# Strided and local attention with a gated feed-forward layer on one core: early loads held back to 1.1 MB under way, and fewer filler products

## The chip, the cores and the metric

The kernel runs on one core of one Trainium2 chip. Its engines are TensorE (PE; its weight loads are shown as PEld), VectorE (DVE), ScalarE (ACT), GpSimd (POOL) and SyncE (SP), which here issues all transfers between HBM and the core's memory. The metric is the device time of one execution in microseconds (us).

## The reference

For 8 batches and 8 heads of 576 positions by 64, the reference computes softmax attention under a mask, four heads with a local band of 32 positions, four with a stride of 32; the heads' outputs, put side by side as x (576 x 512 for each batch), go through a gated layer:

```python
scores = np.where(masks, (q @ k.T) / 8, -1e9)
attn = softmax(scores)                       # per head
x = concat_heads(attn @ v)                   # 576 x 512 per batch
h = np.maximum(x @ w_in, 0.0)                # 512 x 1024
u, v = h[..., :512], h[..., 512:]
v_n = (v - mean(v)) / np.sqrt(var(v) + 1e-6)
v_s = einsum("ts,bsd->btd", w_spatial, v_n) + b_spatial[None, :, None]
out = (u * v_s) @ w_out                      # 512 x 512
```

w_in and w_out arrive as 64-bit floats, the rest as 32-bit.

## The kernel before

All large products are made of two-part operands: each number is split into a rounded part and a rest, and three products of the parts stand for one. So each weight and each activation passes through a short preparation before PE can use it. A weight of 64 bits is loaded as raw words, and the helper `words` (from line 773) turns them into 32-bit numbers in three steps: ACT scales the upper words (L789), POOL or DVE takes three bits of the lower ones (L798), DVE joins them (L806). Then `rnd` writes the rounded part (L412 on ACT, L414 on POOL) and `rest` the remainder (L422). The spatial weights wsp and wtail need only the last two.

A batch has four attention tiles of two heads each. For each tile PE makes scores (L507 for local heads, L650 for strided ones), DVE and ACT the softmax (L527 to L588, L675 to L704), the turned probabilities are copied to ptl or pts, PE multiplies them with v (L617, L720), and ACT and DVE write the result x in two parts (L434, L422). Per batch PE then makes the v half (L957) and the u half (L999) of the first layer, the spatial product (L1079, with its tail in L1091 and L1092) and the last product (L1168).

The order of all this is not written by hand. Each step is entered into a list with a key and a cost, `Program.order` (line 190) plays the list through with costs and latencies, and gives each engine's order and a planned time in ns for each step. The first eight attention tiles and all weights are entered first, so that the loads of the first 50 to 70 us are q, k, v, w_in, w_spatial and w_out mixed. Below, transfers are numbered by their place in SP's order, from 1; the first 53 are issued within the first 66 us of the profile.

Each engine works through its instructions in order and waits at each for the semaphores that it names. A transfer adds to one of eight semaphores, DMAHW0 to DMAHW7, taken in turn: transfer n uses number (n − 1) mod 8. Before a semaphore is taken again, SP waits for the landing of the transfer that had it last, the eighth before; so at most eight are under way.

`Program.fillers` (line 318) looks in the planned first 110 us for places at which PE would stand idle for over 0.7 us ahead of certain steps. There `emit` puts products of a 32x256 tile of zeros (L1349) ahead of the step, into the tile that the step will overwrite: a share, WARM_SHARE, of the idle time divided by 427 ns, rounded down.

```python
if gap > WARM_GAP:
    found[n] = int(WARM_SHARE * gap / WARM_COST)
```

Of the kernel before, what the change touches and what calls it, by code (L numbers as in the profile page):

```python
# [56 lines left out]
    "p": (2.79, 10.51, 0.21,),  # L57
    "b": (25.62, -1.03, 29.44, -12.2, 10.78, 11.69, 33.63, 25.64, -64.18, 15.47, 14.89,),
}
WARM_END, WARM_GAP, WARM_COST, WARM_COLS, WARM_SHARE = 110000.0, 700.0, 427.0, 256, 0.8  # L60
PE_MASKED, APART = (0, 1, 2, 3), (0, 1)
OTHER_BANK = (1, 2, 3)
FETCHED, FETCH_COST = 100.0, 32.0
SLOWED = ((0.3, 0.15), (0.45, 0.6), (0.9, 0.8))
DMA_RATE, DMA_ISSUE, DMA_LAG, DMA_TAIL, TABLE_LOAD = 370.0, 470.0, 1500.0, 500.0, 1280.0
PROD = ((0, 0), (0, 1), (1, 0))
BLOCKS = ("a11", "a12", "a22", "s1", "s2", "s3", "s4")
# [4 lines left out]
PE, ACT, DVE, POOL, DMA = "tensor", "scalar", "vector", "gpsimd", "sync"  # L72
# [77 lines left out]
class Program:  # L150
# [39 lines left out]
    def order(self):  # L190
# [17 lines left out]
        def shared(n, e, at, cost):  # L208

            if e in self.port.get(n, ()):  # L210
                since, until, share, _ = held_by[peer[e]]
                if since <= at < until:
                    both = min(until - at, cost)
                    slow = SLOWED[max(share, self.share[n])]
                    return (slow[0] * both, slow[1] * both) if e == DVE else (slow[1] * both, slow[0] * both)
# [115 lines left out]
                free = at + cost  # L331
        return found

    def emit(self, nc, warm):
        issued = self.order()
        fillers = self.fillers(issued)
        for _, n, e in issued:
            if e == PE and fillers.get(n):
                warm(self.spare[n][1], fillers[n])
            self.ops[n][2](getattr(nc, e))  # L340


def pe_cost(m, n):
# [4 lines left out]
def attention_moe(ctx, tc, qT, kT, ks, vl, vs, cst, eye, w_in, w_out, wsp, wtail, out):  # L348
    nc = tc.nc
# [4 lines left out]
    prog = Program()  # L354
# [898 lines left out]
    starts, knots, at = [], [(0.0, NHP)], 0.0  # L1253
# [98 lines left out]
                start=True, stop=True,  # L1352
            )

    prog.emit(nc, warm)


def _layout(q, k, v, w_in, w_spatial, b_spatial, w_out):
# [75 lines left out]
```

## Time and profile before

| | |
|---|---|
| time, median of 3 runs (lowest, highest) | 520.41 us (519.15, 520.59) |
| the profiled execution: time | 519.78 us |
| the profiled execution: span, first to last instruction | 517.7 us |
| PE busy | 499.6 us, 97% of the span |
| DVE busy | 363.0 us, 70% |
| ACT busy | 267.4 us, 52% |
| POOL busy | 129.0 us, 25% |
| bytes moved | 52.65 MB, 102 GB/s on average |
| mean granted PE clock | 0.98 |

Busy times come from one profiled execution. A timeline row has the start in us, the duration, the engine, the line, the operation, output<-inputs by the program's names without buffer numbers, the shapes and a count; in brackets stands how long the engine was idle before it, and what ended that. A row of SPq is the issue of a transfer. In the view of one tile, the row "DMA to landing" gives the time from issue to landing. L12 is line 12 of the kernel file. The changed file is longer: its lines are ten further down from `emit` on, so that L442, L789 and L1079 are L452, L799 and L1089 there.

### The profile page before, as it was taken

What the parts mean: (1) busy time and instruction counts of PE and PEld (TensorE: products, weight loads), DVE (VectorE), ACT (ScalarE), POOL (GpSimd) and SP (SyncE); (2) the same over time, 40 slices, a digit from 0 to 9 for tenths busy, and PEclk for the clock granted to TensorE, in tenths of its full rate; (3) what the DMA queues carried; (4) which work ended last, traced back from release to release, by engine and by line L of the source; (5) the groups of instructions that cost most, each with busy time, mean ns of one, the idle gap of its engine ahead of it and who ended that gap; (6) DMA issues with size and microseconds to landing.
All of it is one profiled execution on the core that took longest, in us unless ns stands there. A gap on an engine that the chain in (4) does not pass through costs nothing.

```text
span 517.7 us, 14663 instructions
## 1 busy us (share of the span) xinstructions
PE 499.6 (97%) x5884; PEld 459.3 (89%) x5884; DVE 363.0 (70%) x1093; ACT 267.4 (52%) x825; POOL 129.0 (25%) x245
## 2 busy tenths in 40 slices
PE   6779889999999999999999999999999999999997
PEld 3558779979999899998999899998999889998997
DVE  2899989969479747896369764897457861676156
ACT  5786765568554476456336276366446252233222
POOL 3355864043212121312102111233102120102000
PEclk9689979999999999999999999999999999999999
DMA  8897323454024322262023422063011300020002
GB/s 274 307 343 268 125 83 90 149 164 151 2 79 151 118 79 81 85 180 84 11 69 121 148 80 80 1 209 113 1 56 53 123 1 1 1 80 13 1 1 91
DMA packets 26243, 52.65 MB, mean 102 GB/s; under 512 B 3136, under 2 KB 11584, under 8 KB 26176
## 3 DMA queue, kind: packets, MB, share of 16 engines
q1 hardware_dynamic: 26176, 51.72, 30.3%
q8 instruction: 46, 0.75, 0.6%
q14 instruction: 21, 0.17, 0.1%
HBM read 42.27 MB, written 9.44 MB: 100 GB/s over the span
## 4 chain that ended last, share of the span: by engine, by line
PE 89%; DVE 4%; DMA 2%; ACT 2%; SPq 1%; POOL 1%; issue 1%; POOLq 0%
PE m L1079 20%; PE m L957 18%; PE m L1168 18%; PE m L999 18%; PE po L720 4%; PE po L617 3%; PE s L507 3%; PE s L650 2%; PE m L1091 2%; PE m L1092 2%; DMA k<-kT 1%; SPq L442 1%; DMA x<-wsp 1%; PE po L1349 1%; DVE w_in_sb L422 0%
## 5 line engine op out<-in xcount | busy, mean ns | idle before, releaser
L1079 PE MATMUL m<-wsp_sb,vn 128*128 128x288 f32 x768 | 113.3, 300 | 4.3 <-DVE wsp_sb L422 4.3
L1079 PEld LDWEIGHTS m<-wsp_sb,vn 128*128 128x128 f32 x768 | 107.3, 192 | 5.4 <-DVE wsp_sb L422 4.6
L999 PE MATMUL m<-x,w_in_sb 128*128 128x288 f32 x768 | 105.3, 297 | 0.0
L999 PEld LDWEIGHTS m<-x,w_in_sb 128*128 128x128 f32 x768 | 103.4, 188 | 1.2
L957 PE MATMUL m<-w_in_sb,x 128*128 128x512 f32 (+1 forms) x408 | 99.5, 399 | 0.0
L957 PEld LDWEIGHTS m<-w_in_sb,x 128*128 128x128 f32 (+1 forms) x408 | 74.5, 186 | 19.0 <-DVE x L422 0.2
L1168 PE MATMUL m<-g,w_out_sb 128*128 128x288 f32 x384 | 56.9, 298 | 0.0
L414 POOL TENSOR_SCALAR ptl<-pc 32x64 f32<-32x64 f32 (+3 forms) x89 | 37.9, 426 | 64.7 <-DVE pc L588 24.2
L1168 PEld LDWEIGHTS m<-g,w_out_sb 128*128 128x128 f32 x384 | 52.3, 188 | 1.0 <-ACT vv L434 0.3
L422 DVE TENSOR_TENSOR x<-po,x 128x288 fp32r<-128x288 f32 x64 | 27.6, 447 | 36.3 <-ACT x L434 35.6
L1101 DVE TENSOR_TENSOR u<-m,u 128x288 f32<-128x288 f32 x64 | 28.1, 453 | 30.9 <-PE m L1092 30.7
L564 ACT ACTIVATE pl<-pl,ml 128x64 f32<-128x64 f32 (+1 forms) x140 | 47.0, 339 | 4.7 <-DVE ml L544 4.3
L915 ACT ACTIVATE vv<-m 128x512 f32<-128x512 f32 (+1 forms) x37 | 22.0, 596 | 45.7 <-PE m L957 39.6
L412 ACT CAST g<-u 128x288 fp32r<-128x288 f32 x46 | 19.2, 434 | 50.2 <-DVE u L1101 49.0
L933 POOL TENSOR_TENSOR bn<-bn,sel 128x1 f32<-128x1 f32 (+1 forms) x37 | 21.1, 575 | 95.0 <-DVE bn L928 77.0
L1013 ACT ACTIVATE u<-m 128x288 f32<-128x288 f32 x64 | 25.7, 408 | 35.0 <-PE m L999 34.6
L1168 PE MATMUL m<-vn,w_out_sb 128*128 128x288 f32 x288 | 42.6, 297 | 0.0
L920 DVE BATCH_NORM_STATS2 bn<-vv 128x6 f32<-128x512 f32 (+1 forms) x37 | 25.3, 683 | 21.0 <-ACT vv L915 20.5
L1168 PEld LDWEIGHTS m<-vn,w_out_sb 128*128 128x128 f32 x288 | 39.5, 188 | 0.4
L434 ACT CAST x<-po 128x288 fp32r<-128x288 f32 x64 | 24.7, 397 | 26.2 <-PE po L617 14.4
L412 ACT COPY ptl<-pc 32x64 f32<-32x64 f32 (+3 forms) x103 | 35.7, 346 | 4.7 <-DVE pc L588 2.6
L422 DVE TENSOR_TENSOR g<-u,g 128x288 fp32r<-128x288 f32 x64 | 27.0, 449 | 7.9 <-ACT g L412 6.2
(131 smaller groups left out, 726.6 us busy)
## 6 DMA issues: line engine op xcount, KB each, us to landing
q<-qT SPq DMA_DIRECT2D x30, 295.0 KB, 4.2
outT<-o SPq DMA_DIRECT2D x48, 144.0 KB, 2.7
v_raw<-vs SPq DMA_DIRECT2D x13, 512.0 KB, 4.2
v_raw<-vl SPq DMA_DIRECT2D x16, 384.0 KB, 3.7
k<-kT SPq DMA_DIRECT2D x16, 304.0 KB, 4.5
kbd<-ks SPq DMA_DIRECT2D x32, 144.0 KB, 4.6
outT<-vv SPq DMA_DIRECT2D x16, 144.0 KB, 3.7
vn<-w_in SPq DMA_DIRECT2D x4, 512.0 KB, 4.5
```

The lines of the kernel that those rows point to most:

```text
L412: eng.copy(dst(), src())
L414: eng.tensor_scalar(dst(), src(), 1.0, 0.0, op0=ALU.mult, op1=ALU.add)
L422: eng.tensor_tensor(dst(), src(), f32(hi()), op=ALU.subtract)
L434: eng.copy(dst(), src())
L564: eng.activation(p_sb()[:m, u, :], src, AF.Exp, bias=st()[:m, u : u + 1], scale=SCALE if masked else -1.0, **total,)
L920: lambda eng: eng.bn_stats(bn()[:m, 0:6], v()[:m]), [(v,)], [(bn,)],
L957: eng.matmul(v_ps()[:m, :], x_at(kt)[:, a, :], w_in_sb[:, w, kt, HF:], start=(n == 0 and i == 0), stop=(n == NT - 1 and i == 2),)
L999: eng.matmul(u_ps()[:, :HS], w_in_sb[:, w, kt, f * P : (f + 1) * P], xs[NHP * b + kt]()[:, a, r], start=(n == 0 and i == 0), stop=(n == NT ...
L1013: lambda eng, u=u, f=f, u_ps=u_ps: eng.activation(u()[:, f * HS : (f + 1) * HS], u_ps()[:, :HS], AF.Relu),
L1079: eng.matmul(s_ps()[:, :HS], vn()[:, a, kt, fs], wsp_sb[:, w, kt, r], start=(kt == 0 and i == 0), stop=False,)
L1101: lambda eng, ug=ug, s_ps=s_ps: eng.tensor_tensor(ug(), s_ps()[:, :HS], ug(), op=ALU.mult),
L1168: eng.matmul(o_ps()[:, :HS], w_out_sb()[:, b_at, w, kk, a * P : (a + 1) * P], at(j, kk), start=first and kk == 0 and i == 0, stop=kk == 1 ...
```

## The change

Two things are changed. First, WARM_SHARE goes from 0.8 to 0.4. Second, `emit` keeps a list of the transfers sent so far. For each transfer that the plan puts into the first 70 us it goes backwards through the list, the transfer itself included, as long as the sizes come to at most GATE, 1.1 million bytes. The transfer before those it makes a dependency: the new transfer is issued only when that one has landed. No step changes its engine or its place.

```diff
-WARM_END, WARM_GAP, WARM_COST, WARM_COLS, WARM_SHARE = 110000.0, 700.0, 427.0, 256, 0.8
+WARM_END, WARM_GAP, WARM_COST, WARM_COLS, WARM_SHARE = 110000.0, 700.0, 427.0, 256, 0.4
...
+GATE, GATE_END = 1.1e6, 70000.0
...
-    def emit(self, nc, warm):
+    def emit(self, nc, warm, wait):
         issued = self.order()
         fillers = self.fillers(issued)
-        for _, n, e in issued:
+        sent = []
+        for at, n, e in issued:
             if e == PE and fillers.get(n):
                 warm(self.spare[n][1], fillers[n])
-            self.ops[n][2](getattr(nc, e))
+            made = self.ops[n][2](getattr(nc, e))
+            if e == DMA and at < GATE_END:
+                sent.append((made, self.bytes[n]))
+                under_way, k = 0, len(sent)
+                while k and under_way + sent[k - 1][1] <= GATE:
+                    k -= 1
+                    under_way += sent[k][1]
+                if 0 < k < len(sent):
+                    wait(made, sent[k - 1][0])
...
-    prog.emit(nc, warm)
+    def wait(later, earlier):
+        tc.add_manual_dep(
+            later.ins if hasattr(later, "ins") else later, (earlier.ins if hasattr(earlier, "ins") else earlier).name,
+            mybir.DependencyInfo(mybir.DependencyClass.Sync, mybir.DependencyReason.DATA),
+            reason="transfers under way",
+        )
+
+    prog.emit(nc, warm, wait)
```

SP's order at the start, transfers 5 to 14, before. Names are the buffers that are filled (vn and u hold raw words of w_in here, w_out_sb holds an early q) and the inputs; 128x1024 are four-byte words, so w_in's and vs's transfers have 512 KB, vl's 384, kT's 304, qT's 295, wsp's and wtail's 288, ks's 144:

```order
L442 DMA vn_101<-w_in 128x1024
L442 DMA kbd<-ks 64x576 [waits Pool_49]
L442 DMA kbd<-ks 64x576
L442 DMA q_123<-qT 128x590
L442 DMA k_134<-kT 128x608 [waits DMAHW0_49]
L442 DMA v_raw_140<-vl 128x768 [waits DMAHW1_49]
L442 DMA q_176<-qT 128x590 [waits DMAHW2_49]
L442 DMA k_181<-kT 128x608 [waits DMAHW3_49]
L442 DMA v_raw_220<-vl 128x768 [waits DMAHW4_49]
L442 DMA u_225<-w_in 128x1024 [waits DMAHW5_49]
```

The same ten transfers in the changed kernel:

```order
L452 DMA vn_101<-w_in 128x1024 [waits DMAHW1_49]
L452 DMA kbd<-ks 64x576 [waits Pool_49]
L452 DMA kbd<-ks 64x576
L452 DMA q_119<-qT 128x590 [waits DMAHW4_49]
L452 DMA k_130<-kT 128x608 [waits DMAHW0_49]
L452 DMA v_raw_136<-vl 128x768 [waits DMAHW6_49]
L452 DMA q_172<-qT 128x590 [waits DMAHW7_49,DMAHW2_49]
L452 DMA k_177<-kT 128x608 [waits DMAHW3_49,DMAHW0_49]
L452 DMA v_raw_216<-vl 128x768 [waits DMAHW1_49]
L452 DMA u_221<-w_in 128x1024 [waits DMAHW5_49,DMAHW3_49]
```

Nothing has changed its place. Transfer 5 now waits for transfer 2 (DMAHW1), 8 for 5 (DMAHW4), 10 for 7, 11 for 8, 12 for 9 (DMAHW0), 13 for 10 and 14 for 12 (DMAHW3); where two are named, the other is the eighth before, as it was.

SP's order further on, transfers 37 to 44, before (g holds raw words of w_out, xt and v_raw the values v, x raw spatial weights):

```order
L442 DMA g_649<-w_out 128x1024 [waits DMAHW4_49,DVE_49,Pool_49]
L442 DMA k_657<-kT 128x608 [waits DMAHW6_49,DMAHW5_49,PE_49]
L442 DMA q_673<-qT 128x590
L442 DMA kbd<-ks 64x576 [waits DMAHW7_49]
L442 DMA kbd<-ks 64x576 [waits DMAHW0_49]
L442 DMA xt_696<-vs 128x1024 [waits DMAHW1_49]
L442 DMA x_328<-wsp 128x576 [waits DMAHW2_49]
L442 DMA g_736<-w_out 128x1024 [waits DMAHW3_49,DVE_49,Pool_49]
```

And in the changed kernel (the two kbd rows print as one):

```order
L452 DMA g_643<-w_out 128x1024 [waits DMAHW2_49,DVE_49,Pool_49]
L452 DMA k_651<-kT 128x608 [waits DMAHW5_49,DMAHW3_49,PE_49]
L452 DMA q_667<-qT 128x590 [waits DMAHW4_49]
L452 DMA kbd<-ks 64x576 x2
L452 DMA xt_690<-vs 128x1024 [waits DMAHW6_49,DMAHW1_49]
L452 DMA x_322<-wsp 128x576 [waits DMAHW7_49]
L452 DMA g_730<-w_out 128x1024 [waits DMAHW1_49,DVE_49,Pool_49]
```

Transfer 37 now waits for 35 (DMAHW2), 39 for 37 (DMAHW4), 42 for 39 (DMAHW6) and 44 for 42 (DMAHW1).

PE's order ahead of the first value product of a strided tile (s are scores, po the product's tile, pts the turned probabilities), before:

```order
L507 MATMUL s_128<-k_181,q_176 32x64
L507 MATMUL s_131<-k_181,q_176 32x64
L1349 MATMUL po_292<-zeros 32x256 x3
L720 MATMUL po_292<-pts,xt_87 64x4x18 [waits DMAHW1_49,Activation_49,Pool_49]
L720 MATMUL po_292<-pts,xt_87 64x4x18 x7
```

And in the changed kernel:

```order
L517 MATMUL s_124<-k_177,q_172 32x64
L517 MATMUL s_127<-k_177,q_172 32x64
L1359 MATMUL po_288<-zeros 32x256
L730 MATMUL po_288<-pts,xt_87 64x4x18 [waits DMAHW1_49,Activation_49,Pool_49]
L730 MATMUL po_288<-pts,xt_87 64x4x18 x7
```

Here three products on zeros become one. At the start of the program eight become four; there are no others.

## The prediction

> **What bounds the kernel now.** I read the page first, then the busy times by stage, then PE's timeline around the seam between the stages, then ACT's, POOL's and DVE's timelines for the instructions that consume what was loaded, and last single transfers from issue to landing. The page gives the span, and the rate of the transfers in 40 slices of 12.9 us each:
>
> ```profile
> span 517.7 us, 14663 instructions
> ...
> GB/s 274 307 343 268 125 83 90 149 164 151 2 79 151 118 79 81 85 180 84 11 69 121 148 80 80 1 209 113 1 56 53 123 1 1 1 80 13 1 1 91
> ```
>
> The first four slices move about 300 GB/s, all later ones at most 209. The change touches the stage in which memory is asked for most. The profiled execution took 519.78 us for this span, so 2.1 us lie around it; the median of the three runs shown is 520.41, 0.6 above. My sum is made against 519.78.
>
> The stages, from the table of busy times (stretch and its length, then each engine's busy time with its count, granted clock, share of the DMA engines, GB/s):
>
> ```profile
> 0.00:17.00 17.00, 10.35 (x235) 6.47 (x236) 5.09 (x16) 9.83 (x23) 5.20 (x15) 0.81 0.88 306
> 17.00:53.40 36.40, 32.77 (x518) 25.99 (x517) 34.87 (x86) 27.90 (x78) 20.16 (x33) 0.90 0.83 292
> 53.40:67.20 13.80, 9.54 (x63) 8.15 (x61) 13.80 (x43) 10.62 (x34) 11.95 (x15) 0.93 0.36 127
> 67.20:517.70 450.50, 446.94 (x5071) 418.66 (x5071) 309.21 (x952) 219.09 (x692) 91.71 (x184) 0.99 0.24 78
> ```
>
> After 67.2 us PE is busy for 446.9 of 450.5 us: whatever delays the start of that stage delays the end, and there is no idle time in which to win it back. Before it, DVE is the full engine: 34.9 of 36.4 us, then 13.8 of 13.8. The seam itself, in PE's timeline:
>
> ```profile
> 62.64 0.29 PE L1079 MATMUL m<-wsp_sb,vn 128*128 128x288 f32 x1
> 67.21 3.01 PE L1079 MATMUL m<-wsp_sb,vn 128*128 128x288 f32 x11 [4.28 <-DVE wsp_sb L422]
> ```
>
> PE stands idle for 4.28 us until DVE has made wsp_sb. So the question is by how much the change moves DVE's work before 67.2 us, and that work starts from loaded data. These instructions consume loads first (start, duration, engine, line):
>
> ```profile
> 26.36 0.67 ACT L789 ACTIVATE g<-g 128x512 f32<-128x512 f32 x1
> 34.22 0.68 ACT L789 ACTIVATE u<-u 128x512 f32<-128x512 f32 x1
> 38.41 0.67 ACT L789 ACTIVATE vn<-vn 128x512 f32<-128x512 f32 x1
> 43.91 0.67 ACT L789 ACTIVATE g<-g 128x512 f32<-128x512 f32 x1
> 51.88 0.70 ACT L789 ACTIVATE g<-g 128x512 f32<-128x512 f32 x1
> 57.21 0.66 ACT L412 CAST wt_b<-x 128x576 fp32r<-128x576 f32 x1
> 52.48 0.67 POOL L798 TENSOR_SCALAR g<-g 128x512 int32<-128x512 uint8 x1
> 53.36 1.17 DVE L806 SCALAR_TENSOR_TENSOR g<-g 128x512 int32<-128x512 int32 x1
> ```
>
> They are the users of transfers 21, 29, 33, 37, 44 and 49 (numbered as SP issues them); POOL's and DVE's rows are the next steps on transfer 44.
>
> **The change, part by part.** *The wait.* A transfer may now be issued only when it and those still unlanded come to at most 1.1 MB, 1,074 KB of 1,024 bytes. So what counts is how long a transfer takes from issue to landing with little ahead of it. Single transfers that were issued into an idle queue, or nearly so:
>
> ```profile
> L442 SPq DMA_DIRECT2D w_out_sb<-qT x1: 387/387/387, 0.7 to 0.7; - x1
> DMA to landing us min/median/max: 3.0/3.0/3.0
> ...
> L442 SPq DMA_DIRECT2D g<-w_out x1: 327/327/327, 64.1 to 64.1; - x1
> DMA to landing us min/median/max: 3.5/3.5/3.5
> ...
> L442 SPq DMA_DIRECT2D kbd<-ks x1: 477/477/477, 22.1 to 22.1; - x1
> DMA to landing us min/median/max: 2.4/2.4/2.4
> ...
> L442 SPq DMA_DIRECT2D q<-qT x1: 328/328/328, 89.0 to 89.0; - x1
> DMA to landing us min/median/max: 3.4/3.4/3.4
> ...
> L442 SPq DMA_DIRECT2D v_raw<-vs x1: 328/328/328, 215.4 to 215.4; - x1
> DMA to landing us min/median/max: 4.6/4.6/4.6
> ...
> L442 SPq DMA_DIRECT2D xt<-vs x1: 416/416/416, 1.2 to 1.2; - x1
> DMA to landing us min/median/max: 3.8/3.8/3.8
> ```
>
> So 295 KB take 3.0 us (3.4 at worst), 512 KB 3.5 (4.6 at worst), 144 KB 2.4. While the queue was full it moved this much:
>
> ```profile
> 12.00:20.00 8.00, 5.28 (x122) 2.86 (x110) 5.88 (x17) 4.72 (x19) 2.15 (x4) 0.50 1.03 405
> ```
>
> At 405 GB/s, 405 thousand bytes per us, 512 KB need 1.3 us and 295 KB 0.75: about 2.2 us of every lone landing is not movement. With up to eight transfers under way, as before, those 2.2 us are hidden behind other transfers. With 1,074 KB they are mostly not, since the sizes fit badly: 512+304+295 is 1,111, and 512+512+144 is 1,168.
>
> The new waits can be followed by hand. I go through the order of issue, adding sizes backwards until they pass 1,074 KB, and keep only the transfers that wait for one another in a row. Transfer 2 (512 KB) lands at 1.2 + 3.8 = 5.0 us. Transfer 5 (512 KB) waits for it: 8.5. Transfer 8 (295) waits for 5: 11.5; 9 (304), issued right behind it, lands 0.8 later: 12.3. Transfer 12 (304) waits for 9: 15.3; 14 (512) for 12: 18.8; 16 (295) for 14: 21.8; 19 (512) for 16: 25.3; 21 (512) for 19: 28.8. Then 24, 26 and 29 (512 each): 32.3, 35.8, 39.3; 31 (304): 42.3; 33 (512): 45.8; 35 (304): 48.8; 37 (512): 52.3; 39 (295): 55.3; 42 and 44 (512 each): 58.8 and 62.3. From transfer 5 on that is eleven links of 3.5 us, six of 3.0 and the 0.8, 57.3 us on top of 5.0. Between the landings of 12 and 44 lie 11.3 MB, so the rate falls to 11.3 MB / 47 us = 240 GB/s, where the table has 292.
>
> Set against the users: transfer 21 comes at 28.8 for an ACT instruction that now starts at 26.4 (2.4 late), 29 at 39.3 for 34.2 (5.1 late), 33 at 45.8 for 38.4 (7.4), 37 at 52.3 for 43.9 (8.4), 44 at 62.3 for 51.9 (10.4). The lateness grows at each, so none is a consequence of the one before: the transfers set the pace, and ACT, POOL and DVE, which take their instructions in order, stand still behind each. Behind ACT's waiting instruction stand the evacuations of x and the copies of ptl and pts, for which PE waits; behind SP's waiting issue stand the later loads alone, since the stores of results come after the gated stretch.
>
> At transfer 44 the path leaves the queue. POOL starts on it 62.3 − 52.5 = 9.8 us later, and DVE's L806 with it. From there DVE has 13.8 us of work in 13.8 us, so PE's restart at 67.2 moves by the same 9.8. Transfer 49 (waits for 46, which waits for 44) comes still a little later for wt_b, but ACT has 10.6 busy of 13.8 us there and makes it up. PE's work ahead of the seam moves too and ends 4.28 us before it, which covers a PE that runs some of it at a lower clock.
>
> The rows of a lone landing scatter upwards only. If about one in five of the eleven large links takes 4.6 instead of 3.5, that adds 11/5 × 1.1 = 2.4. I take 9.8 + 2.4 = 12.2 us. Bounds: the 144 KB row has 2.4 − 0.36 of movement, 2.0 instead of 2.2 us; with that all 17 links come 0.17 shorter, 2.9 in all, and the delay is 6.9. With half of the links at their longest (5.5 × 1.1 + 3 × 0.4 = 7.3) it is 17.1.
>
> The Trainium skill (DMA: Bandwidth & Descriptors, section "Anatomy of one DMA — SWDGE (gpsimd) path") fits a DMA as 2.0 us plus its bytes at 436 GB/s, for another issuing path than SP's. By that a 512 KB link would be an estimated 3.2 us and a 295 KB link 2.7, 17 × 0.3 = 5.1 us less, and the time would be about 524.5 without the one-in-five; the trace's own rows, 3.5 and 3.0, are higher and I go by them.
>
> *The products on zeros.* Eleven become five: eight to four at the start, three to one ahead of the first value products (the counts are rounded down). PE's row of the second group, what follows it, and the makers of pts:
>
> ```profile
> 16.78 2.77 PE L1349 MATMUL po<-zeros 128*32 128x256 f32 x6
> 19.48 1.88 PE L720 MATMUL po<-pts,xt 128*64 128x72 f32 x32
> ...
> 15.62 0.92 POOL L414 TENSOR_SCALAR pts<-pc 32x288 f32<-32x288 f32 x2 [7.84 <-DVE pc L704]
> ...
> 16.04 0.86 ACT L412 COPY pts<-pc 32x288 f32<-32x288 f32 x2
> ...
> 20.75 0.40 ACT L434 CAST x<-po 128x288 fp32r<-128x288 f32 x1 [0.64 <-PE po L720]
> 21.41 0.40 ACT L434 CAST x<-po 128x288 fp32r<-128x288 f32 x1 [0.25 <-PE po L720]
> ```
>
> pts is complete at 16.9, so the three products (2.77 us, two rows each) hold L720 back by about 2.5 us; with one, 1.8 us of that go. I cost the gain at nothing, because ACT, which evacuates L720's result, then waits for transfer 21 until 28.8 in any case. Without that cover it would be worth the 0.64 + 0.25 = 0.9 us that ACT idles there. The four products dropped at the start lie in a wait for loads. That PE's clock may be lower for longer, bounded by the 0.50 of the row 12 to 20, also falls into waits.
>
> Sum: 519.78 + 12.2 − 0 = 532.0 us.
>
> **The rivals.** *Faster: landings come sooner because less is under way.* Transfer 16 needed three times as long as a lone one of its size, behind up to seven others, and PE waited for a k:
>
> ```profile
> L442 SPq DMA_DIRECT2D w_out_sb<-qT x1: 706/706/706, 10.0 to 10.0; - x1
> DMA to landing us min/median/max: 9.4/9.4/9.4
> ...
> PE s L507 <- DMA k<-kT: 1.3, 1, 1.3
> ```
>
> If the time that is not movement is itself made by the crowd, a queue with 1.1 MB lands each as soon as its bytes are moved, PE's early loads come earlier, and L720 too. It decides if a 512 KB link costs less than 2.9 us: the 9.8 us spread over 17 links are 0.58 each. Then the waits are free, the products give 0.9 and PE's wait for k at most 1.3: 519.78 − 2.2 = 517.6 us. Against it: the lone rows above have no crowd and none is under 3.5. The Trainium skill says something of this kind (same page, section "Latency and other measured facts"): HBM access takes 0.2 us on average and 2 at high load, so that a lighter load means a smaller fixed cost. The lone rows do not bear that out.
>
> *No change: the slack takes it.* Not every load is used as it lands; ACT rounds one of the last gated ones, transfer 51, only here:
>
> ```profile
> 65.58 0.67 ACT L412 CAST wsp_sb<-x 128x576 fp32r<-128x576 f32 x1
> ```
>
> If the links come out near 2.9 us, the users above get their data about when they get it now, and the seam holds: 519.8 ± 1. Against it: five users in a row are late by growing amounts, and the lone rows lie above 2.9.
>
> *Slower still: every link at its long end.* 11 × 1.1 + 6 × 0.4 = 14.6 on top of 9.8: 544 us. For it: in the gated stretch one or two other transfers are always being issued and moved; against it: half of the lone rows sit at the short end.
>
> That the wait is not in the program is no rival, since SP's listing has it.
>
> **How the numbers follow.** A measurement of this kernel can tell about 0.3% (1.6 us) from no change. My forecast, 532.0, gets 0.85; the longer tail 0.08; no change 0.03; the faster rival 0.04. The range runs from the short links (519.78 + 6.9 = 526.7, rounded down to 526) to half of them long (519.78 + 17.1 = 536.9, rounded up to 538). Slower by over 0.3%: 0.85 + 0.08 = 0.93.
>
> **What would show it.** In the changed kernel's profile the first five slices should stand near 240 GB/s and the sixth should still be full; transfer 44 should land near 62 to 65 us; ACT should wait for a DMA ahead of each L789 (L799 there); PE's stage of the spatial products should start near 79 instead of 67.2 and last 450 us as before. I am wrong if 512 KB land in under 3 us there, if ACT's waits on loads do not grow from one to the next, or if PE starts that stage before 70.

## The result, and the profile after

| kernel | median | lowest and highest of 6 runs | profiled run | its span |
|---|---|---|---|---|
| before | 519.14 us | 517.61 to 520.59 | 519.78 us | 517.7 us |
| changed | 535.04 us | 533.55 to 535.77 | 535.77 us | 533.9 us |

The ratio is 1.0302, with a 95% interval of 1.0277 to 1.0326: the change makes the kernel 15.9 us slower. The forecast was 532.0 us, in a range of 526 to 538.

The changed kernel's page, its span and its rate of transfers in 40 slices of 13.3 us:

```profile
span 533.9 us, 14639 instructions
...
GB/s 223 212 231 216 199 195 114 79 153 154 116 2 99 168 108 85 32 116 221 1 77 3 257 41 50 66 109 205 0 55 0 169 2 1 1 56 34 1 1 88
```

The first four slices stood near 300 GB/s before and stand near 220 now, and the stretch of heavy loading reaches to the sixth slice, some 80 us, where it was four slices. The stages; the first two are cut at the same times as before, the last at 82.40 us, 0.7 us ahead of the seam (length, busy time of PE, weight loads, DVE, ACT and POOL with counts, granted clock, DMA share, GB/s):

```profile
0.00:17.00 17.00, 8.70 (x154) 5.65 (x155) 5.01 (x15) 8.71 (x21) 4.58 (x14) 1.00 0.69 225
17.00:53.40 36.40, 27.44 (x434) 20.48 (x434) 22.40 (x51) 19.86 (x53) 12.53 (x23) 0.81 0.67 218
...
82.40:533.90 451.50, 445.20 (x5071) 416.50 (x5071) 309.97 (x953) 220.33 (x696) 91.93 (x184) 1.00 0.24 78
```

The last stage holds the same 5071 matmuls and lasts as long as it did (451.5 us from 82.40 and 450.8 from the seam, and 450.5 before). DVE, busy for 34.9 of 36.4 us before, has 22.4 of 36.4 here: it waits. The time is lost ahead of the seam, and the seam in PE's timeline shows how much:

```profile
83.10 6.46 PE L1089 MATMUL m<-wsp_sb,vn 128*128 128x288 f32 x47 [1.68 <-DVE wsp_sb L432]
```

PE restarts at 83.10 us instead of 67.21, 15.9 us later, and that is the whole loss.

The chain of waits, from the start of the gated stretch to the first engine in it (start, duration, what; rows of under 0.1 us are left out):

```profile
1.17 3.86 DMA xt<-vs
5.05 3.52 DMA vn<-w_in
8.59 0.33 SPq L452
8.97 3.33 DMA k<-kT
12.32 4.57 DMA k<-kT
16.90 3.51 DMA u<-w_in
20.43 3.83 DMA w_out_sb<-qT
24.32 3.88 DMA w_out_sb<-vs
28.21 3.49 DMA g<-w_in
31.72 4.37 DMA vn<-w_in
36.16 3.89 DMA v_raw<-vs
40.07 4.73 DMA u<-w_in
44.82 2.73 DMA k<-kT
47.56 3.41 DMA vn<-w_in
50.99 3.18 DMA k<-kT
54.25 3.93 DMA g<-w_out
58.19 2.81 DMA q<-qT
61.06 3.86 DMA xt<-vs
65.00 3.46 DMA g<-w_out
68.51 4.06 DMA v_raw<-vl
72.63 2.80 DMA x<-wtail
75.46 0.67 ACT wt_b L422
```

No computing engine stands in it until 75 us. One transfer begins where another ends: 2, 5, 9, 12, 14, 16, 19, 21, 24 and so on to 42 and 44, which lands at 68.46 us (51.86 before), then 46 and 49. ACT's waits for loads, in total, times and longest:

```profile
ACT g L799 <- DMA g<-w_out: 8.2, 2, 4.3
ACT u L799 <- DMA u<-w_in: 7.6, 2, 5.2
ACT vn L799 <- DMA vn<-w_in: 6.7, 2, 4.0
...
ACT g L799 <- DMA g<-w_in: 2.6, 1, 2.6
...
ACT wt_b L422 <- DMA x<-wtail: 1.9, 1, 1.9
```

Six of these eight waits are those of the users of transfers 21, 29, 33, 37, 44 and 49, which the prediction named; the other two are for transfers 5 and 14. In the order of the transfers the waits of the first five are 2.6, 5.2, 4.0, 3.8 and 4.3 us.

### The profile page after: what moved, and what is told of

The parts are those of the page before. It is cut to its first block, busy times and chain, and to the rows that moved or that the text cites. A ratio compares the mean times of both kernels' runs of the same rounds, so it can differ in the third digit from the quotient of the medians.

```text
span 533.9 us, 14639 instructions
## 1 busy us (share of the span) xinstructions
PE 503.1 (94%) x5872; PEld 460.8 (86%) x5872; DVE 358.3 (67%) x1093; ACT 267.0 (50%) x825; POOL 128.5 (24%) x245
## 4 chain that ended last, share of the span: by engine, by line
PE 82%; DMA 14%; ACT 2%; DVE 1%; issue 1%; SPq 0%
PE m L1089 18%; PE m L1178 17%; PE m L967 17%; PE m L1009 17%; PE po L730 3%; PE po L627 3%; DMA k<-kT 3%; DMA vn<-w_in 2%; PE s L517 2%; PE s L660 2%; DMA u<-w_in 2%; PE m L1101 2%; PE m L1102 1%; DMA xt<-vs 1%; DMA g<-w_out 1%
## 5 line engine op out<-in xcount | busy, mean ns | idle before, releaser
L1089 PE MATMUL m<-wsp_sb,vn 128*128 128x288 f32 x768 | 111.3, 296 | 2.8 <-DVE wsp_sb L432 1.7
L1089 PEld LDWEIGHTS m<-wsp_sb,vn 128*128 128x128 f32 x768 | 105.2, 189 | 4.4 <-DVE wsp_sb L432 2.2
L1009 PE MATMUL m<-x,w_in_sb 128*128 128x288 f32 x768 | 106.9, 299 | 1.5 <-ACT vv L925 1.4
L967 PE MATMUL m<-w_in_sb,x 128*128 128x512 f32 (+1 forms) x408 | 104.5, 413 | 1.9 <-ACT u L1023 1.9
L967 PEld LDWEIGHTS m<-w_in_sb,x 128*128 128x128 f32 (+1 forms) x408 | 77.6, 193 | 22.5 <-ACT u L1023 2.1
L424 POOL TENSOR_SCALAR ptl<-pc 32x64 f32<-32x64 f32 (+3 forms) x89 | 38.3, 430 | 55.7 <-DVE pc L598 20.8
L444 ACT CAST x<-po 128x288 fp32r<-128x288 f32 x64 | 24.7, 398 | 22.4 <-PE po L627 12.0
L950 DVE TENSOR_SCALAR vv<-vv,bn 128x512 f32<-128x512 f32 (+1 forms) x37 | 21.4, 578 | 18.0 <-POOL bn L943 17.6
```

Of the source, the lines that this page charges most:

```text
L424: eng.tensor_scalar(dst(), src(), 1.0, 0.0, op0=ALU.mult, op1=ALU.add)
L444: eng.copy(dst(), src())
L967: eng.matmul(v_ps()[:m, :], x_at(kt)[:, a, :], w_in_sb[:, w, kt, HF:], start=(n == 0 and i == 0), stop=(n == NT - 1 and i == 2),)
L1009: eng.matmul(u_ps()[:, :HS], w_in_sb[:, w, kt, f * P : (f + 1) * P], xs[NHP * b + kt]()[:, a, r], start=(n == 0 and i == 0), stop=(n == NT ...
L1089: eng.matmul(s_ps()[:, :HS], vn()[:, a, kt, fs], wsp_sb[:, w, kt, r], start=(kt == 0 and i == 0), stop=False,)
```

## The experiments

The theory: the limit of 1.1 MB turns the early loads into a row of links, each of them a fixed part of some 2 us plus the bytes that lie ahead, so the loads set the pace and the end moves with transfer 44. The rivals: the loss is that of the products on zeros, through the clock or through TensorE's time; or it is the number of bytes kept back that counts, and not the links; or only the last loads ahead of the seam count. Each kernel is the changed one with one or two constants, or one constant and one condition, altered. A limit of 1e12 makes no wait; a share of 0.8 gives the eleven zero products of before, 0.4 five, 0.0 none. Each run is compared with runs of the kernel before on the same chip.

**Five zero products without the waits.**

```
-GATE, GATE_END = 1.1e6, 70000.0
+GATE, GATE_END = 1e12, 70000.0
```

> The filler half of the change alone: five products on zeros instead of eleven, no new waits. Queue theory (the new waits do it all, each gated transfer paying its full time from issue to landing): within 0.9 us of before, ratio 0.998 to 1.002, L720 starting about 1.8 us earlier than 19.5. Clock rival (a share of the 15.9 us comes from a colder PE after fewer products on zeros): slower than before by more than 2 us.

Measured: 519.5 us, ratio 1.0011 (0.9994 to 1.0027). Halving the zero products does nothing that can be told from no change. L720 (L730 there) starts at 18.82 us, 0.7 earlier than before and not 1.8; the rows for this stand further down.

**The waits with eleven zero products.** It was run twice.

```
-WARM_END, ..., WARM_SHARE = 110000.0, 700.0, 427.0, 256, 0.4
+WARM_END, ..., WARM_SHARE = 110000.0, 700.0, 427.0, 256, 0.8
```

> The waits alone at 1.1 MB, with all eleven products on zeros. Queue theory: 15 to 17 us slower than before, as the whole change (ratio 1.029 to 1.033), since PE then only fills waits. Clock rival: clearly less than the whole change, under 14 us.

Measured: 534.2 us, ratio 1.0288 (1.0254 to 1.0323), with transfer 44 landing at 68.26 us; the second time 533.22 us, 1.0272 (1.0254 to 1.029). The seam lies at 82.87 us in the first run, 0.23 from the changed kernel's. In the second run's profile transfer 44 lands at 66.17 us and the seam lies at 80.55: the row of the same program is 2 us shorter in one execution than in another. Of these 2.3 us at the seam only 0.9 are left in the time of the two profiled executions (534.48 and 533.54), since the 47 products behind the seam took 8.00 us in the first and 9.10 in the second. The waits make the loss by themselves, but for at most some 1.6 us: the second ratio is 0.003 under the changed kernel's, 14.4 us where I expected 15 to 17, and the intervals overlap.

**Other limits.** Five kernels have the eleven zero products and another limit; of each diff one line is shown.

```
+GATE, GATE_END = 1.2e6, 70000.0
```

> The waits alone with the limit at 1.2 MB instead of 1.1. Queue theory, that sizes just miss the limit: 512+304+295 KB and 512+512+144 KB now fit, so many transfers wait for one further back, the row of waits gets shorter, transfer 44 lands near 59 us instead of 68.5, and the loss falls by about half, to 6 to 9 us (ratio 1.012 to 1.018). Rival, that waiting as such costs, in proportion to how tight the limit is: 15.9 x 1.1/1.2 = 14.6 us.

```
+GATE, GATE_END = 1.4e6, 70000.0
```

> The waits alone with the limit at 1.4 MB. Queue theory: enough under way to cover about 2.4 us that are not movement, the early loads land about when they are needed, loss 0 to 3 us (ratio 1.000 to 1.006). Rival, cost in proportion to the limit: 15.9 x 1.1/1.4 = 12.5 us (ratio 1.024).

```
+GATE, GATE_END = 0.6e6, 70000.0
```

> Limit 600 KB (so one transfer of 512 KB at a time), eleven zero products as before the change. Theory (a link of the row is a fixed part of about 2.4 us from the end of one transfer to the first bytes of the next, plus the bytes that lie ahead): with nothing under way beside it, a 512 KB transfer takes about 3.5 us and the next one begins only behind it, so the row has all large transfers in it and not every second one; the rate falls to about 140 GB/s, transfer 44 lands near 120 us instead of 68.5, and the time is about 590 us (575 to 605). Rival (the loss goes as the number of bytes kept from being under way, 15.9 us at 1.1 MB, in proportion): about 548 us (540 to 560).

```
+GATE, GATE_END = 2.2e6, 70000.0
```

> Limit 2.2 MB (some four large transfers), eleven zero products. Queue theory: a link of four large transfers takes about 2.4 us and 2.2 MB at some 400 GB/s, so the rate is about 280 to 320 GB/s; 519 to 522 us (0 to +3). Rival (a transfer that is not crowded serves its user sooner, and the kernel before has too many under way): faster than the kernel before by more than 1.5 us, under 517.4 us.

```
+GATE, GATE_END = 1.7e6, 70000.0
```

> Limit 1.7 MB (three large transfers), eleven zero products. Queue theory: between the 6.1 us that 1.4 MB costs and the nothing that 2.2 MB costs, and as late as transfer 44 lands; 520 to 523 us (+1 to +4), transfer 44 at 53 to 56 us. Rival (a step: as soon as a link's fixed part is covered by one further large transfer the waits are free): within 0.5 us of the kernel before.

Measured, in the order of the limits (the rate is that of the stretch from 12 to 58 us; the seam is the start of the 47 matmuls on L1089; "none" is the kernel before, with the rows of its profile):

| limit | median | ratio and interval | GB/s, 12 to 58 | transfer 44 lands | seam |
|---|---|---|---|---|---|
| none (before) | 519.14 | 1 | 301 | 51.86 | 67.21 |
| 2.2 MB | 519.45 | 0.9988 (0.9974 to 1.0002) | 301 | 51.03 | 67.08 |
| 1.7 MB | 519.36 | 1.0005 (0.9991 to 1.0019) | 297 | 52.97 | 67.42 |
| 1.4 MB | 524.54 | 1.0118 (1.0085 to 1.015) | 263 | 58.58 | 73.01 |
| 1.2 MB | 528.63 | 1.0197 (1.0168 to 1.0227) | 249 | 62.34 | 76.98 |
| 1.1 MB | 534.2 | 1.0288 (1.0254 to 1.0323) | 224 | 68.26 | 82.87 |
| 1.1 MB, second time | 533.22 | 1.0272 (1.0254 to 1.029) | 232 | 66.17 | 80.55 |
| 0.6 MB | 588.29 | 1.1324 (1.1297 to 1.135) | 133 | 114.59 | 135.79 |

The limit of 0.6 MB settles it between the theory (about 590) and proportion (about 548): 588.3. That it came so near to 590 is in part luck: transfer 44 landed at 114.59 and not near 120, and the chain stayed in the queue for 14 us more, to the landing of 49 at 128.57. The limit of 2.2 MB, where a rival had a gain of over 1.5 us, gave none that can be told from no change. The run at 0.6 MB also shows each transfer with nothing large beside it. Its transfers from 0 to 131 us, by tile (engine, operation, count, KB each, median us from issue to landing):

```profile
k<-kT SPq DMA_DIRECT2D x6, 304.0 KB, 2.7
v_raw<-vl SPq DMA_DIRECT2D x4, 384.0 KB, 2.9
kbd<-ks SPq DMA_DIRECT2D x10, 144.0 KB, 2.5
...
u<-w_in SPq DMA_DIRECT2D x2, 512.0 KB, 3.4
...
g<-w_out SPq DMA_DIRECT2D x2, 512.0 KB, 3.4
...
v_raw<-vs SPq DMA_DIRECT2D x1, 512.0 KB, 4.4
```

And the same of the changed kernel, from 5 to 73 us:

```profile
k<-kT SPq DMA_DIRECT2D x6, 304.0 KB, 3.8
v_raw<-vl SPq DMA_DIRECT2D x4, 384.0 KB, 4.1
kbd<-ks SPq DMA_DIRECT2D x10, 144.0 KB, 3.3
u<-w_in SPq DMA_DIRECT2D x2, 512.0 KB, 4.1
...
g<-w_out SPq DMA_DIRECT2D x2, 512.0 KB, 3.7
```

With room for a second transfer the medians are 0.3 to 1.2 us longer. This fits a link that carries not only its own bytes but what is left of those ahead.

The limits of 1.2 and 1.4 MB cost more than I expected (10.2 and 6.1 us by the table's ratios, where I had 6 to 9 and 0 to 3) and less than the rival gave. At 1.2 MB I had counted the links that remain at their old length. Its chain has 14 of them from transfer 5 to 44, where the changed kernel has 17, but of 4.1 us on average and not 3.7; three are of 384 KB (3.7 to 5.1 us), which take the place of loads of about 300 KB. At 1.4 MB the 512 KB loads took 4.7 us (median of ten), and the chain leaves the queue at 45.06 us for the engines and comes back with transfer 44 at 54.39, so its loss is not that of a row throughout. The limit of 1.7 MB cost nothing, where I expected 1 to 4 us; it came out as the rival, a step, had it.

From 12 to 58 us the kernel before moves 301 GB/s, and 1.7 MB under way carry 297, so hardly any load is late. Between 1.4 and 1.7 MB the limit stops being felt. A limit divided by the rate that it allows is an upper bound of the time that a byte's place in the queue is taken, since less than the limit can be under way: 1.1 MB at 224 GB/s is 4.9 us, 1.4 MB at 263 is 5.3, 1.7 MB at 297 is 5.7, where the rate is nearly what the stage asks for. With some 5.5 us, 301 GB/s need about 1.7 MB under way, an estimate from these rows; the times show only that it lies between 1.4 and 1.7.

**The limit on one part of the loads.** With eleven zero products, the waits are made for the first 25 transfers alone, or from transfer 26 on alone; of the diffs the condition is shown.

```
-                if 0 < k < len(sent):
+                if 0 < k < len(sent) <= 25:
```

> The limit of 1.1 MB for the first 25 transfers alone, eleven zero products. Queue theory: the early row of links (up to the v of the second head, transfer 24) ends as in the changed kernel, about 4 to 5 us late at 36 us, then the free queue makes up a part; 522 to 525 us (+3.5 to +5). Rival (only the last transfers ahead of the spatial products count, since the engines have slack before them): no more than +1 us.

```
-                if 0 < k < len(sent):
+                if 0 < k < len(sent) and len(sent) > 25:
```

> The limit of 1.1 MB from transfer 26 on alone, eleven zero products. Queue theory: the row begins where the free queue has transfer 26 and goes on with the links of the changed kernel; transfer 44 lands 7 to 10 us late, 526 to 529.5 us (+7 to +10), so that with the run of the first 25 alone it adds up to about the whole +15 us. Rival (the last transfers alone count): +13 to +15 us, and the run of the first 25 shows nothing.

Measured: 524.25 us, ratio 1.0091 (1.0075 to 1.0108), for the first 25; 526.7 us, 1.014 (1.012 to 1.0159), from 26 on. Both lie in the bands of the theory, and the early waits count by themselves, so the rival with the last loads alone is out. But 4.9 and 7.4 us make 12.3, not the 15 of both together. The first kernel's rates show why:

```profile
12.00:41.00 29.00, 19.92 (x415) 14.69 (x416) 19.60 (x46) 17.74 (x53) 10.94 (x21) 0.77 0.76 251
41.00:58.00 17.00, 14.71 (x240) 12.30 (x240) 14.37 (x48) 11.84 (x34) 9.56 (x13) 1.00 0.94 350
```

Once its queue is free it moves 350 GB/s, and transfer 44, after transfer 24 came 7.9 us late (35.34, and 27.46 before; I expected 4 to 5), is 3.4 late (55.26). With the limit on throughout there is no such free stretch, and nothing is made up.

**No zero products at all**, without the waits and with them. The share is 0.0 in both; the first also has the limit of 1e12. The third text is that of the second run with the waits and eleven zero products.

```
+WARM_END, ..., WARM_SHARE = 110000.0, 700.0, 427.0, 256, 0.0
```

> No products on zeros at all and no waits for transfers. Theory (they lie beside other work and no granted clock hangs on them): 518.5 to 520.5 us, within 1 us of the kernel before. Rival (they hold up TensorE's clock): the early products run slower and the end is 2 to 5 us later. Second rival (they take TensorE's time): faster by over 1 us.

> The waits at 1.1 MB as in the changed kernel, and no products on zeros. If the waits cover the zero products (TensorE waits for transfers anyway), the same as the waits with eleven, within 1 us: 533 to 536 us. Rival (without cover, the 0.9 us between the changed kernel and the waits alone are the price of six products removed): 1.5 to 2 us over the waits with eleven, 535.5 to 537 us.

> The waits at 1.1 MB with all eleven products on zeros, a second time, beside the run without any: 533 to 535.5 us. If the zero products cost nothing either way, it and the run without any differ by under 1 us.

Measured without the waits: 517.11 us, ratio 0.9971 (0.9958 to 0.9984), 1.5 us faster than before, which misses my band; the second rival has the sign and about the size. With the waits: 533.71 us, 1.028 (1.0259 to 1.0301), beside 533.22 with eleven; no difference, as expected. The changed kernel, with five, has 535.04: more than either, so the order is not that of the products, and no price of theirs can be read from it. The start of L730 in PE's timeline of the kernel without zeros and waits:

```profile
17.63 2.38 PE L730 MATMUL po<-pts,xt 128*64 128x72 f32 x32 [1.91 <-POOL pts L424]
```

The same place with five zero products and no waits:

```profile
17.47 0.43 PE L517 MATMUL s<-k,q 64*32 64x64 f32 x5 [2.08 <-issue]
17.83 1.06 PE L1359 MATMUL po<-zeros 128*32 128x256 f32 x2
18.82 2.19 PE L730 MATMUL po<-pts,xt 128*64 128x72 f32 x32
```

With none, L730 starts as soon as pts is there, at 17.63; with five it starts at 18.82, and with eleven at 19.48. In the five-product kernel PE pauses for 2.08 us inside its scores with nothing to wait for in the profile, so that much of what the two dropped products gave back was lost again ahead of them. That the zero products lie on the path in the kernel before can be read from its chain of waits:

```profile
16.85 2.70 PE po L1349 x6
19.55 1.84 PE po L720 x32
```

With the waits at 1.1 MB this place is no longer in the chain, which consists of transfers there, and the zero products cost nothing. The kernel without zero products and waits is the fastest of all that were run. No zero products together with a limit of 1.7 MB was not tried.

## Why the prediction was right, and which term was too small

*After 67.2 us a delay of the seam is a delay of the end.* Right: the seam moved by 15.9 us and the median by 15.9, and over the other limits of the table the seam and the time move together, within some 1.3 us.

*The limit makes a row of links.* Right, link for link: the chain of waits is the row that was worked out by hand. The run at 0.6 MB, with 588 us, leaves no room for proportion.

*The length of a link* is the term that was mis-sized. The row was to bring transfer 44 in at 62.3 us, with 2.4 more allowed for long links, and the sign was a landing between 62 and 65; it landed at 68.46. Of the 6.2 us, the eleven links of 512 KB make 3.6 (they add up to 42.05 us, where eleven of 3.5 are 38.5), the six of about 300 KB with the pair 2.0 (20.8 for 18.8, from the issue of 8 to the landing of 9 for the pair), and the rest, some 0.6, lies between one landing and the next issue in the chain, which I had at nothing. The step that failed is "if about one in five of the eleven large links takes 4.6 instead of 3.5". For lone transfers it is nearly right: in the run at 0.6 MB two of the thirteen of 512 KB from transfer 5 to 44 took 4.4 us (both load vs, as the row of 4.6 did) and eleven 3.4 to 3.6. In the changed kernel six of the eleven links took 3.9 to 4.7 and five 3.4 to 3.5. Every one of the eleven had another transfer under way beside it, so the medians above show that company makes transfers longer, but not which of them. I had priced every link by rows of transfers into an idle queue, while the limit leaves room for two. In the second run with the waits and eleven zero products the same row ended at 66.17, 2.3 us sooner, so a part of the 6.2 is scatter between executions.

One of those rows was not of an idle queue: transfer 22 (144 KB, 2.4 us) was issued at 22.09, and transfer 21 landed at 23.47. Alone, at 0.6 MB, its size took 2.5 us, so the bound made with it stands. The upper bound of the range was worked out as 536.9 and written as 538; the measured time lies under either.

The Trainium skill (DMA: Bandwidth & Descriptors, section "Anatomy of one DMA — SWDGE (gpsimd) path") gives 2.0 us plus the bytes at 436 GB/s, for another issuing path than SP's, which makes an estimated 3.2 us of 512 KB, 2.7 of 304 and 2.3 of 144. The medians of the lone transfers at 0.6 MB, 3.4 to 3.5 for weights of 512 KB, 2.7 and 2.5, agree within 0.3 us; the two loads of 4.4 do not. Where it was used as the length of a link, in the 524.5 us that the forecast set beside its own, it was 10.5 us short of the median, for the same reason as my rows.

*At transfer 44 the path leaves the queue.* Wrong, though it cost the sum little. I had ACT make up the lateness of transfer 49. The chain stays in the queue for 46 and 49, 7.0 us more, and then runs through ACT. From the landings of 44 and of 49 to the seam in the changed kernel (columns as in the stages above):

```profile
68.46:83.10 14.64, 10.31 (x55) 7.47 (x53) 12.73 (x42) 11.93 (x38) 13.71 (x16) 0.88 0.58 179
75.44:83.10 7.66, 4.41 (x14) 2.28 (x14) 7.00 (x26) 7.46 (x21) 6.96 (x9) 0.78 0.40 118
```

And from the landing of 44 in the kernel before:

```profile
51.86:67.21 15.35, 11.08 (x75) 9.69 (x73) 15.35 (x46) 12.15 (x38) 13.34 (x17) 0.94 0.41 139
```

Before, DVE (third) is busy without a gap, 15.35 of 15.35 us. After, it is so for 12.73 of 14.64, and ACT (fourth) is the full one, 7.46 of the 7.66 us behind transfer 49. The stretch from 44 to the seam came to 14.64 us, 0.7 under the old one, and so shifting the seam by transfer 44's delay gave nearly the right answer for a partly wrong reason, which is luck.

*ACT's waits grow from one to the next.* They do not (2.6, 5.2, 4.0, 3.8, 4.3 us), though this was named as a sign of being wrong. What grows is the lateness, as the prediction had it: transfers 21, 29, 33, 37 and 44 let ACT start 5.4, 10.6, 12.6, 14.4 and 16.6 us later than before. ACT comes late to each load already, having waited for the one before, so a single wait is not the lateness, and the sign was badly chosen.

*The halved zero products at nothing.* Right for this change: without the waits no difference from 0, and with them none between eleven and none. The price without cover, 0.9 us, is not borne out for six of them: it would be a ratio of 0.9983, and the interval without the waits begins at 0.9994. All eleven cost 1.5 us.

*The rivals.* Landings that come sooner because less is under way: the 512 KB links would have had to fall below 2.9 us, and the shortest took 3.41. The Trainium skill's rule beside it (same page, section "Latency and other measured facts"), by which a lighter load has a smaller fixed cost, is not seen here: at the lightest load, 0.6 MB, weights of 512 KB took 3.4 to 3.5 us, as much as the shortest of the lone rows before (3.5). No change through slack: ACT waited for eight loads, and PE for k and kbd. All links long, 544 us: six of the eleven were, and the time went about a quarter of the way from the forecast to it.

## What to carry to other kernels

In this kernel a limit on the bytes under way was free at 1.7 MB and cost 6.1 us at 1.4. For another kernel, a first estimate of where it becomes free is the rate that the stage asks for, times the time that a transfer holds its place (here 301 GB/s and some 5.5 us, about 1.7 MB). Well below that, as at 1.1 MB here, the loads become a row of links, each with its fixed part bare, and whatever stands behind them moves by the sum. To price such a row, take the link's length from transfers with as much ahead of them as the limit leaves, not from lone ones, and follow the row to the last load that the seam needs. A filler that is meant to keep an engine ready is itself work and is worth a run without it.

## What was not expected of the hardware

The granted clock in the rows and the length of the matmuls can disagree. The first products of L967 at 20 to 28 us (count, minimum, median and maximum in ns) and the stretch from 26 to 28 us (columns as in the stages, the granted clock third from the end), first in the changed kernel, then in the one with the waits and no zero products:

```profile
L967 PE MATMUL m<-w_in_sb,x x3: 628/628/797, 26.8 to 27.8; 128*128 128x512 f32 x3
...
26.00:28.00 2.00, 2.00 (x62) 1.73 (x52) 1.08 (x4) 0.47 (x2) 0.20 (x1) 0.50 0.90 346
```

```profile
L967 PE MATMUL m<-w_in_sb,x x3: 628/629/797, 26.6 to 27.6; 128*128 128x512 f32 x3
...
26.00:28.00 2.00, 2.00 (x47) 1.67 (x39) 1.28 (x5) 0.75 (x4) 0.02 (x1) 1.00 0.73 290
```

They are equally slow, where the same products take 388 and 387 ns at best later on. Yet the granted clock there is 0.50 in the first kernel and 1.00 in the second, which shows 1.00 in every stretch up to 28 us. So the high clock of the kernels without zero products (1.00 from 12 to 20 us, where the kernel before has 0.50) is no proof that taking them away lifts the clock, and the 1.5 us gained are put down to their place on the path alone, as far as these runs go. What makes PE pause inside its scores, 1.45 us with eleven and 2.08 us with five, stays open; the kernel with none has no such pause there.
